# Fused attention, soft mixture of experts and gated MLP: 15 KB more for weights, another order of heads, early clamps on GpSimd

## The chip, the cores and the metric

The kernel runs on one core of a Trainium2 chip. The metric is device time in microseconds, the median of the runs shown. All times of the trace are counted from the first instruction of the profiled execution.

## The reference

Three layers follow each other, all in float32. Attention has 4 batches, 8 heads, 576 tokens and head size 64. Heads 0 to 3 are local (a token sees itself and 31 before it), heads 4 to 7 strided (it sees earlier tokens with the same position modulo 32).

```python
scores = scale * np.matmul(q, k.transpose(0, 1, 3, 2))
scores = np.where(masks[None], scores, -1e9)
attn = softmax(scores);  x = attn @ v            # 2304 tokens x 512

logits = x @ phi                                 # 2304 x 32 slots
slot_input = softmax(logits, axis=0).T @ x       # 32 slots, 4 per expert
slot_out[e] = relu(slot_input[e] @ w1[e]) @ w2[e]    # 8 experts, 512-1024-512
x = softmax(logits, axis=1) @ slot_out

g = x @ w_gate                                   # 512 x 1536
out = (g * sigmoid(g) * (x @ w_val)) @ w_out     # 1536 x 512
```

`w_gate`, `w_val` and `w_out` come as float64; the kernel makes float32 of their bits by itself.

## The kernel before, in words

**Attention.** Two batches at a time (a batch pair, `bp`) and one head make a unit: 16 units, in the order of `HORDER` (heads 0, 1, 4, 5, 2, 3, 6, 7) for both pairs. A unit has three steps of three blocks of 64 tokens. The loop at line 612 takes two steps, n and n+1, in one pass. In pass n TensorE computes the scores of steps n and n+1 (`qk`, line 297, into two banks in turn), the products with v of steps n-4 and n-3 (`pv`, 335) and the transposes of the weights of steps n-2 and n-1 (`tr`, 322). VectorE adds masks and takes maxima (line 303), later divides (341 to 350, writes x); ScalarE takes exponentials (315) and copies transposes (325). Work that comes once per pair of heads hangs at fixed steps in the tables `early`, `side` and `late`: the x-transposes `xtr` (361, with ScalarE's copies 362), the logits (381, a bank per batch pair; strided heads read x with a step), and after the last logits of a batch pair the exponentials over tokens and the slot products `slot` (446). After the last unit a tail of dependent small steps leads to the slot inputs (`weights_a`, `weights_b`, `slot_in`), and the first expert product needs these.

**Loads.** SyncE's queue issues all loads in program order. When the third step of unit u is multiplied with v, `load_v(u + 3)` and `load_qk(u + 4)` are issued and weight halves up to `WTO[u]` (`load_to`, line 635; the list `loads`, line 154, has 70 halves of 512 KB). `load_v` also puts three copies of v on GpSimd (line 278), which shift it to other partitions. Weights lie in `NB` = 14 buffers of two halves; `SHARED` weights go to the buffers of q, k and v when these are done with, `SPEC` weights to buffers of x (tag "x", 6 of them), `SPLIT` to two other places. In the first expert product (line 656, order `W1ORDER`) each weight that is used up frees a buffer, and two more halves are issued; then comes the second product (line 745, order `W2ORDER`).

**Early conversions.** Three tiles of the float64 weights (`PRE`) are loaded first and converted during attention. One conversion (`conv`) has ten parts, in this order: two magnitudes (ScalarE, 198), two clamps (VectorE, 201), two shifts (204), two low words (208), two signs (212, all VectorE). `PRECONV` says at which step how many parts are put at the end of a step's work (`late`): from step 6 on one part a step. So the first conversion has its magnitudes in pass 6, clamps in pass 8, shifts in 10, low words in 12, signs in 14; the second has them in passes 16 to 24, the third from pass 26 to 34.

**Last stage.** The rest of the float64 weights is converted while TensorE multiplies (`half`; its clamp, line 229, is on GpSimd). Program order is the order of each engine's queue.

Of the kernel before, what the change touches and what calls it, by code (L numbers as in the profile page):

```python
# [9 lines left out]
F32 = mybir.dt.float32  # L10
# [4 lines left out]
ALU = mybir.AluOpType  # L15
AX = mybir.AxisListType.X

S = 576
HD = 64
NT = 9  # L20
# [1 line left out]
WID = (96, 80)  # L22
SHIFT = (0, 16)
NEG = -1.0e30
HORDER = (0, 1, 4, 5, 2, 3, 6, 7)
UNITS = [(bp, h) for bp in range(2) for h in HORDER]
C_ID, C_SEL4, C_SELT, C_END = 0, 128, 256, 320
NB = 14
SPEC = (0, 14, 15)
W2ORDER = tuple(range(16, 32, 2)) + tuple(range(17, 32, 2))  # L30
SPLIT = 13
SHARED = W2ORDER[2:5]
WORDER = list(range(1, 11)) + [12, 11] + list(W2ORDER[:2])
REST = list(W2ORDER[5:])
W1ORDER = (1, 2, 3, 4, 0, 13, 5, 6, 7, 14, 8, 15, 9, 10, 12, 11)
PRE = [("g", 0), ("g", 1), ("o", 0)]
PRECONV = [(6, 1), (7, 1), (8, 1), (9, 1), (10, 1), (11, 1), (12, 1), (13, 1), (14, 1), (15, 1), (16, 1), (17, 1), (18, 1), (19, 1), (20, 1), (21, 1), (22, 1), (23, 1), (24, 1), (25, 1), (26, 1), (27, 1), (28, 1), (31, 2), (32, 2), (33, 1), (34, 1), (35, 1)]
ORDER = [("g", 2), ("g", 3), ("o", 1), ("g", 4), ("g", 5), ("o", 2), ("g", 6), ("g", 7), ("o", 3), ("g", 8), ("g", 9), ("g", 10), ("g", 11), ("o", 4), ("o", 5)]
LAG = 3
AHEAD_H = 12  # L40
WT = (0, 0)
ATDVE = ((15, 1),)
# [13 lines left out]
START = (2, 1)  # L56
HEAD = "h g l a0 a1 p2 s0 w1 s1 g p1 w1"
WARM0 = 8
WTO = [6, 8, 10, 12, 14, 16, 18, 20, 22, 24, 26, 28, 31, 38, 42, 43]
NG = 4  # L60
CUTS = [(0, 1, 5, 12), (0, 2, 6, 12), (0, 2, 7, 12), (0, 3, 8, 12), (0, 3, 8, 12)]
MAG_LO = float(np.uint32(0x38000000).view(np.float32))
# [50 lines left out]
def build(ctx: ExitStack, tc: tile.TileContext, cst, phi, qh, kh, vh, w1, w2, wgv, wo, out):  # L113
# [31 lines left out]
    kt = [s0[:, 0:K], s1[:, VW:VW + K], s2[:, VW:VW + K]]  # L145
    vt = [s3[0:96, 0:VW], s1[0:96, 0:VW], s2[0:96, 0:VW]]
    col, par = s2[:, VW + K:VW + K + 128], s2[:, VW + K + 128:VW + K + 144]
    ml, ms = s1[:, VW + K:VW + K + 192], s3[:, VW + S:VW + S + 720]

    wsrc = [w1[j] for j in range(16)] + [w2[j] for j in range(16)]  # L150
    def halves(*js):
        return [(j, hf) for j in js for hf in range(2)]

    loads = halves(*PRE, *WORDER, SPEC[0], *SHARED, SPLIT, *SPEC[1:], *REST)
    at_spec = loads.index((SPEC[0], 0))
    at_split = loads.index((SPLIT, 0))
    wt, gt = {}, {}
# [3 lines left out]
    def load_half(k):  # L161
        for _ in range(k):
            if wn[0] >= NW:
                return
            j, hf = loads[wn[0]]
            if j in SPEC:
                wt[j, hf] = ap_.tile([128, 1024], F32, tag="x", name="wx", bufs=6)
            elif j == SPLIT:
                wt[j, hf] = ap_.tile([128, 2, S], F32, tag="xT", name="wx", bufs=1).rearrange("p a b -> p (a b)")[:, 0:1024] if hf else tmp[:, 0:1024]
            elif hf == 0:  # L170
                a = shared[SHARED.index(j)] if j in SHARED else wp.tile([128, 2048], F32, tag="w", name="w", bufs=NB)
                if j in PRE:
                    gt[j] = a.bitcast(I32)
                wt[j, 0], wt[j, 1] = a[:, 0:1024], a[:, 1024:2048]
            if j in PRE:
                o, i = wt[j, hf].bitcast(I32), (wgv if j[0] == "g" else wo)[j[1], hf].bitcast(I32)
            else:
                o, i = wt[j, hf], wsrc[j][hf]
            SP.dma_start(out=o, in_=i)
            wn[0] += 1  # L180
# [6 lines left out]
    def conv(kind, j):  # L187
        src = gt[kind, j]
        if kind == "g":
            dst = wg[j] = wgs[j % len(wgs)]  # L190
        else:
            dst = wof[j] = wos[j % len(wos)]
        v = [src[:, 1024 * k:1024 * k + 1024].rearrange("p (n t) -> p n t", t=2) for k in range(2)]
        d = [dst[:, 512 * k:512 * k + 512] for k in range(2)]
        di = [a.bitcast(I32) for a in d]

        def mag(k):
            ACT.activation(out=d[k], in_=v[k][:, :, 1].bitcast(F32), func=AF.Abs)

        def clamp(k):  # L200
            DVE.tensor_scalar(out=d[k], in0=d[k], scalar1=MAG_LO, scalar2=MAG_HI, op0=ALU.max, op1=ALU.min)

        def shift(k):
            DVE.tensor_scalar(out=di[k], in0=di[k], scalar1=3, scalar2=0x3FFFFFFF, op0=ALU.logical_shift_left,
                              op1=ALU.bitwise_and)

        def low(k):
            DVE.scalar_tensor_tensor(out=di[k], in0=v[k][:, :, 0], scalar=29, in1=di[k],
                                     op0=ALU.logical_shift_right, op1=ALU.bitwise_or)

        def sign(k):
            DVE.scalar_tensor_tensor(out=di[k], in0=v[k][:, :, 1], scalar=-0x40000000, in1=di[k],
                                     op0=ALU.bitwise_and, op1=ALU.bitwise_or)

        return [(c, fn, k) for c, fn in ((0.0, mag), (0.34, clamp), (0.34, shift), (0.6, low), (0.6, sign))
                for k in range(2)]
# [90 lines left out]
    def expo(u, t):  # L307
        W = WID[UNITS[u][1] // 4]
        sm, mx = sc.pop((u, t))
        o = 288 * ((3 * u + t) % 2)  # L310
        e = tmp[:, o:288 + o].rearrange("p (j k) -> p j k", j=3)
        if W < 96 and u % 4 == 2 and t < 2:
            DVE.memset(e[:, :, 0:96 - W], 0.0)
        for j in range(3):
            ACT.activation(out=e[:, j, 96 - W:96], in_=sm[:, j, 0:W], func=AF.Exp, scale=-1.0, bias=mx[:, j:j + 1])  # L315
        ex[u, t] = e
# [11 lines left out]
    def pv(two):  # L328
        ps = bank("pv", 2)
        for n, (u, t) in enumerate(two):  # L330
            a = at.pop((u, t))
            for j in range(3):
                for b in range(2):
                    o = 65 * (3 * n + j)
                    PE.matmul(out=ps[64 * b:64 * b + 64, o:o + 65], lhsT=a[:, j, 64 * b:64 * b + 64],  # L335
                              rhs=vt[u % AHEAD][:, 65 * (NT * b + 3 * t + j):65 * (NT * b + 3 * t + j) + 65],
                              start=True, stop=True, skip_group_check=True)
        k = 3 * len(two)
        p3 = ps[:, 0:65 * k].rearrange("p (j d) -> p j d", j=k)
        dn = ap_.tile([128, 2, 6, 1], F32, tag="dn", name="dn", bufs=2)[:, :, 0:k]  # L340
        DVE.tensor_scalar_add(dn[:, 0], p3[:, :, HD:HD + 1], 1.0e-9)
        DVE.reciprocal(dn[:, 1], dn[:, 0])
        (u, t), (u1, _) = two[0], two[-1]
        for n, u, t, m in [(0, u, t, 3 * len(two))] if u == u1 else [(0, u, t, 3), (3, u1, 0, 3)]:
            bp, h = UNITS[u]
            y = h // 4
            st, e = divmod(h % 4, 2)
            if t == 0 and e == 0:
                xt[bp, y, st] = ap_.tile([128, NT, 128], F32, tag="x", name="x", bufs=6)
            DVE.tensor_tensor(out=xt[bp, y, st][:, 3 * t:3 * t + m, 64 * e:64 * e + 64], in0=p3[:, n:n + m, 0:HD],  # L350
                              in1=dn[:, 1, n:n + m].to_broadcast([128, m, HD]), op=ALU.mult)

# [11 lines left out]

    lg = {}

    def logits(bp, y, st):
        first, last = (y, st) == (0, 0), (y, st) == (1, 1)
        if first:
            lg[bp] = bank("lg", 1)  # L370
        a = xT.pop((bp, y, st))
        for hf in range(2):
            for b in range(2):
                o = 64 * hf + 32 * b
                if y:
                    rhs = a[:, b, :].rearrange("p (r t) -> p t r", t=18)[:, 9 * hf:9 * hf + 9, :]
                    dst = lg[bp][o:o + 32, 0:288].rearrange("p (t r) -> p t r", r=32)
                else:
                    rhs = a[:, b, 288 * hf:288 * hf + 288]
                    dst = lg[bp][o:o + 32, 0:288]  # L380
                PE.matmul(out=dst, lhsT=phi_t[:, 2 * y + st, :], rhs=rhs, start=first, stop=last,  # L381
                          skip_group_check=True)
# [135 lines left out]
    with tc.manual_schedule():  # L518
# [56 lines left out]
        for bp in range(2):  # L575
            for y in range(2):
                for st in range(2):
                    u = 8 * bp + 4 * st + 2 * y + 1
                    at_step(3 * u + (3 if u == 15 else 5), xT_new, bp, y, st)
                    at_step(3 * u + (3 if u == 15 else 5), xtr, bp, y, st, 0)  # L580
                    at_step(3 * u + 5, xtr, bp, y, st, 1, ("tr", 2) if u in (9, 11) else ("ms", 1))
                    (at_step if u == 15 else lambda n, *a: early.setdefault(n, []).append((a[0], a[1:])))(
                        3 * u + (5 if u == 15 else 7), xtr, bp, y, st, 2)
                    at_step(3 * u + 7, logits, bp, y, st)
# [27 lines left out]
        while n < len(steps) or any(k >= n for k in side):  # L612
            two = (n, n + 1)
            for k in two:
                if k < len(steps):
                    u, t = steps[k]
                    qk(u, t)
            if n == 2:
                load_qk(3)
                load_half(2)  # L620
# [384 lines left out]
```

## Time and profile before

| | |
|---|---|
| time, median of 3 runs | 357.6 us (356.43 to 357.95) |
| profiled execution | 356.76 us, span 355.0 us |
| granted clock of TensorE | 1.00 |
| TensorE busy | 338.2 us (95%) |
| VectorE, ScalarE, GpSimd busy | 219.2, 186.0, 132.7 us |
| DMA | 71.94 MB, mean 203 GB/s |

The span reaches from the first to the last instruction. Busy shares are means over stages that differ: attention to 116 us, the expert products to 152 us, the last stage to the end. PE is TensorE, PEld its weight loads, DVE VectorE, ACT ScalarE, POOL GpSimd, SPq SyncE's queue.

### The profile page before, as it was taken

The numbers are of one execution on the slowest core, as the hardware profiler recorded it, in microseconds if no ns is written. First come the engines' busy times: TensorE is split into PE (matmuls) and PEld (weight loads), VectorE is DVE, ScalarE is ACT, GpSimd is POOL, SyncE is SP. The second block draws the span as 40 slices with busy tenths as digits, with TensorE's granted clock in tenths as the row PEclk, the third lists the DMA queues.
The fourth block names the chain that finished last, engine by engine and source line by source line (L and its number), as shares of the span: only waits on it lengthen the run. The fifth ranks groups of instructions, "written<-read, shape, count | busy, mean of one in ns | idle before, by whom it ended". The sixth has DMA issues, their size and how long they took to land.

```text
span 355.0 us, 7690 instructions
## 1 busy us (share of the span) xinstructions
PE 338.2 (95%) x2856; PEld 244.6 (69%) x2856; DVE 219.2 (62%) x707; ACT 186.0 (52%) x449; POOL 132.7 (37%) x163
## 2 busy tenths in 40 slices
PE   8988999899989999989999999999999999999995
PEld 5866776787747553346777767777776887878774
DVE  4977786765646015468777888797858725242532
ACT  3886979756842002376756555565436634333321
POOL 1514313212110020046484665474526763443331
PEclk9999999999999999999999999999999999999999
DMA  7999999959998999993333334342300003030303
GB/s 205 352 365 404 338 373 361 296 195 349 338 411 310 343 409 408 410 380 127 119 120 118 118 120 123 114 139 99 118 2 2 0 2 118 0 120 2 118 34 143
DMA packets 23397, 71.94 MB, mean 203 GB/s; under 512 B 2624, under 2 KB 3520, under 8 KB 23360
## 3 DMA queue, kind: packets, MB, share of 16 engines
q1 hardware_dynamic: 23072, 71.32, 55.0%
q8 instruction: 22, 0.36, 0.4%
q10 hardware_dynamic: 288, 0.14, 0.1%
q14 instruction: 15, 0.12, 0.1%
HBM read 66.73 MB, written 4.72 MB: 201 GB/s over the span
## 4 chain that ended last, share of the span: by engine, by line
PE 66%; DMA 11%; DVE 9%; ACT 7%; issue 3%; SPq 1%; POOL 1%; DVEq 0%; ACTq 0%; POOLq 0%
PE o L859 35%; DMA w<-in_w 8%; PE sc L297 5%; PE pv L335 5%; PE tr L322 4%; PE gv L825 3%; PE gv L826 3%; PE tr L361 2%; PE lg L381 2%; PE ms L446 2%; DMA s<-in_vh 2%; DVE h L832 2%; DMA g<-in_wgv 1%; PE gv L805 1%; ACT tmp L325 1%
## 5 line engine op out<-in xcount | busy, mean ns | idle before, releaser
L842 POOL TENSOR_TENSOR hl<-h,hh 128x512 fp32r<-128x512 f32 (+1 forms) x60 | 70.9, 1182 | 86.9 <-ACT hh L841 86.8
L859 PE MATMUL o<-woh,hh 128*128 128x512 f32 (+1 forms) x220 | 87.7, 399 | 2.6 <-DVE acc L885 1.4
L859 PE MATMUL o<-wol,hh 128*128 128x512 f32 (+1 forms) x220 | 85.1, 388 | 0.0
L832 DVE TENSOR_TENSOR h<-gv,sg 128x512 f32<-128x512 f32 (+1 forms) x59 | 37.5, 635 | 50.2 <-ACT sg L831 47.3
L859 PE MATMUL o<-woh,hl 128*128 128x512 f32 (+1 forms) x220 | 59.4, 386 | 0.0
L841 ACT CAST hh<-h 128x512 fp32r<-128x512 f32 (+1 forms) x60 | 34.6, 577 | 45.4 <-DVE h L832 45.4
L859 PEld LDWEIGHTS o<-woh,hh 128*128 128x128 f32 x220 | 41.3, 188 | 17.4 <-DVE acc L885 3.4
L278 POOL COPY s<-s 32x390 f32<-32x390 f32 (+1 forms) x48 | 24.2, 504 | 66.7 <-DMA s<-in_vh 52.6
L859 PEld LDWEIGHTS o<-woh,hl 128*128 128x128 f32 x220 | 41.1, 188 | 8.7
L831 ACT ACTIVATE sg<-gv 128x512 f32<-128x512 f32 (+1 forms) x60 | 33.1, 554 | 25.9 <-PE gv L825 25.5
L859 PEld LDWEIGHTS o<-wol,hh 128*128 128x128 f32 x220 | 41.4, 188 | 7.6
L315 ACT ACTIVATE tmp<-tmp,mx 128x96 f32<-128x96 f32 (+1 forms) x144 | 40.9, 363 | 3.8 <-DVE mx L303 3.7
L303 DVE CUSTOM_DVE_ANT_0 tmp<-sc,s 128x96 f32<-128x96 f32 (+1 forms) x144 | 27.9, 245 | 16.4 <-PE sc L297 15.1
L297 PEld LDWEIGHTS sc<-s,s 64*64 64x64 f32 x576 | 24.0, 136 | 10.6 <-issue 5.1
L297 PE MATMUL sc<-s,s 64*64 64x96 f32 (+1 forms) x576 | 28.4, 245 | 2.0 <-DVE mx L303 1.4
L325 ACT COPY tmp<-tr 96x384 f32<-96x384 f32 x47 | 20.2, 476 | 18.7 <-PE tr L322 18.6
L825 PE MATMUL gv<-cs,St 128*128 128x512 f32 (+1 forms) x60 | 25.4, 423 | 0.3 <-DVE St L814 0.3
L229 POOL TENSOR_SCALAR wg<-wg 128x512 f32<-128x512 f32 x20 | 12.3, 614 | 29.1 <-DMA g<-in_wgv 25.4
L335 PE MATMUL pv<-s,tmp 96*64 96x65 f32 x576 | 22.4, 225 | 0.3 <-POOL s L278 0.3
L826 PE MATMUL gv<-cs,St 128*128 128x512 f32 (+1 forms) x59 | 22.3, 379 | 0.3 <-DVE St L814 0.2
L335 PEld LDWEIGHTS pv<-s,tmp 96*64 96x64 f32 x576 | 19.0, 137 | 3.7 <-issue 0.7
L322 PE MATMUL tr<-cst_t,tmp 128*96 128x128 f32 x144 | 21.1, 280 | 0.3 <-ACT xT L362 0.3
(167 smaller groups left out, 460.3 us busy)
## 6 DMA issues: line engine op xcount, KB each, us to landing
w<-in_w SPq DMA_DIRECT2D x50, 512.0 KB, 8.3
g<-in_wgv SPq DMA_DIRECT2D x10, 1024.0 KB, 5.0
g<-in_wo SPq DMA_DIRECT2D x5, 1024.0 KB, 4.9
s<-in_vh SPq DMA_DIRECT2D x16, 292.5 KB, 5.8
out<-osb SPq DMA_DIRECT2D x17, 256.0 KB, 2.2
s<-in_qh SPq DMA_DIRECT2D x15, 288.0 KB, 5.9
s<-in_kh SPq DMA_DIRECT2D x15, 288.0 KB, 6.0
wx<-in_w SPq DMA_DIRECT2D x7, 512.0 KB, 5.7
```

Of the source, the lines that this page charges most:

```text
L297: PE.matmul(out=ps[r, W * j:W * j + W], lhsT=qt[u % AHEAD][r, 64 * i:64 * i + 64], rhs=kt[u % AHEAD][r, c0:c0 + W], start=True, stop=True, ...
L303: DVE.tensor_tensor_reduce(out=sm[:, j, 0:W], in0=ps[:, W * j:W * j + W], in1=mask(y, 3 * t + j), scale=-0.125, scalar=3.0e38, op0=ALU.add ...
L315: ACT.activation(out=e[:, j, 96 - W:96], in_=sm[:, j, 0:W], func=AF.Exp, scale=-1.0, bias=mx[:, j:j + 1])
L322: PE.transpose(ps[0:96, 128 * j:128 * j + 128], e[:, j, :], ident)
L335: PE.matmul(out=ps[64 * b:64 * b + 64, o:o + 65], lhsT=a[:, j, 64 * b:64 * b + 64], rhs=vt[u % AHEAD][:, 65 * (NT * b + 3 * t + j):65 * (N ...
L825: PE.matmul(out=pg[:, 0:n], lhsT=St[f][:, 0:128], rhs=csf[:, t0:t0 + n], start=True, stop=True)
L826: PE.matmul(out=pvv[:, 0:n], lhsT=St[f][:, 128:256], rhs=csf[:, t0:t0 + n], start=True, stop=True)
L831: ACT.activation(out=sg[:, 0:n], in_=pg[:, 0:n], func=AF.Silu)
L832: DVE.tensor_tensor(out=h[:, 0:n], in0=pvv[:, 0:n], in1=sg[:, 0:n], op=ALU.mult)
L841: ACT.copy(a, h)
L842: POOL.tensor_tensor(out=l, in0=h, in1=a.bitcast(F32), op=ALU.subtract)
L859: PE.matmul(out=o[:, 0:c], lhsT=(a, a, l)[i][:, 128 * t:128 * t + 128], rhs=(woh, wol, woh)[i][f][:, c * k:c * k + c], start=(first and i ...
```

## The change

The reservation for dynamic DMA descriptors goes from its default to 1024 bytes, which frees 15 KB per partition. `NB` becomes 15 and tag "x" has 7 buffers; one more second-layer weight is loaded early, the lists and `WTO` follow, and one half of `SPEC` is loaded ahead of the `SHARED` weights. The local heads 2 and 3 come last in both batch pairs; the local masks `ml` move from buffer s1 to s0, and the bank of logits is closed by another pair of heads. The clamps of the early conversions go to GpSimd, and all their parts come two steps (one pass) later: first conversion in passes 8 to 16, second in 18 to 26, third from 28 to 36, with its first clamp at step 31, its second clamp and first shift at step 32, its second shift at step 33. Six filler matmuls are put behind the scores of passes 0, 2 and 4.

```diff
-HORDER = (0, 1, 4, 5, 2, 3, 6, 7)
+HORDER = (0, 1, 4, 5, 6, 7, 2, 3)
-NB = 14
+NB = 15
-SHARED = W2ORDER[2:5]
-WORDER = list(range(1, 11)) + [12, 11] + list(W2ORDER[:2])
-REST = list(W2ORDER[5:])
+SHARED = W2ORDER[3:6]
+WORDER = list(range(1, 11)) + [12, 11] + list(W2ORDER[:3])
+REST = list(W2ORDER[6:])
-PRECONV = [(6, 1), (7, 1), ..., (28, 1), (31, 2), (32, 2), (33, 1), (34, 1), (35, 1)]
+PRECONV = [(k, 1) for k in range(8, 29)] + [(31, 2), (32, 2)] + [(k, 1) for k in range(33, 38)]
+FILL = {0: 3, 2: 2, 4: 1}
-WTO = [6, 8, 10, 12, 14, 16, 18, 20, 22, 24, 26, 28, 31, 38, 42, 43]
+WTO = [6, 8, 10, 13, 15, 17, 20, 22, 24, 27, 29, 31, 34, 41, 45, 46]
-    ml, ms = s1[:, VW + K:VW + K + 192], s3[:, VW + S:VW + S + 720]
+    ml, ms = s0[:, K + 2 * S:K + 2 * S + 192], s3[:, VW + S:VW + S + 720]
-    loads = halves(*PRE, *WORDER, SPEC[0], *SHARED, SPLIT, *SPEC[1:], *REST)
+    loads = (halves(*PRE, *WORDER, SPEC[0]) + [(SPEC[1], 0)] + halves(*SHARED, SPLIT) + [(SPEC[1], 1)] +
+             halves(SPEC[2], *REST))
...
-                wt[j, hf] = ap_.tile([128, 1024], F32, tag="x", name="wx", bufs=6)
+                wt[j, hf] = ap_.tile([128, 1024], F32, tag="x", name="wx", bufs=7)
...
         def clamp(k):
-            DVE.tensor_scalar(out=d[k], in0=d[k], scalar1=MAG_LO, scalar2=MAG_HI, op0=ALU.max, op1=ALU.min)
+            POOL.tensor_scalar(out=d[k], in0=d[k], scalar1=MAG_HI, scalar2=MAG_LO, op0=ALU.min, op1=ALU.max)
...
-        if W < 96 and u % 4 == 2 and t < 2:
+        if W < 96 and u % 8 == 2 and t < 2:
             DVE.memset(e[:, :, 0:96 - W], 0.0)
...
-        first, last = (y, st) == (0, 0), (y, st) == (1, 1)
+        first, last = (y, st) == (0, 0), (y, st) == (0, 1)
...
-                    u = 8 * bp + 4 * st + 2 * y + 1
+                    u = 8 * bp + 4 * st + 2 * (y != st) + 1
...
+            if n in FILL:
+                warm(FILL[n])
...
-    nc = bacc.Bacc("TRN2", target_bir_lowering=False, num_devices=1)
+    nc = bacc.Bacc("TRN2", target_bir_lowering=False, num_devices=1, dynamic_dma_scratch_size=1024)
```

## Rows read from the trace of the kernel before

**Rows 1.** Stages: from:to, length, busy (instructions) by engine, PEclk, DMA, GB/s.
```profile
28.50:58.00 29.50, 28.45 (x471) 21.65 (x471) 21.70 (x132) 23.77 (x73) 7.74 (x17) 1.00 1.00 370
...
74.00:92.00 18.00, 17.76 (x313) 13.83 (x311) 10.82 (x81) 11.99 (x40) 2.80 (x6) 1.00 0.75 266
...
131.80:152.00 20.20, 19.98 (x161) 7.92 (x161) 9.14 (x27) 5.22 (x8) 0.00 (x0) 1.00 1.02 405
...
160.00:355.00 195.00, 188.64 (x874) 144.65 (x872) 124.26 (x201) 95.28 (x184) 99.41 (x98) 1.00 0.25 84
```

**Rows 2.** Waits, 116 to 160 us: engine, line, releaser, total, times, longest.
```profile
PEld sc L656 <- issue: 6.7, 30, 0.2
...
PEld pv L745 <- DMA w<-in_w: 2.9, 4, 1.1
```

**Rows 3.** Timeline, second expert product, weight loads: start, duration, operation, [idle before <-releaser].
```profile
142.50 0.13 PEld L745 LDWEIGHTS pv<-w,hz 128*32 128x32 f32 x4 [0.30 <-issue]
...
147.13 0.14 PEld L745 LDWEIGHTS pv<-w,hz 128*32 128x32 f32 x4 [0.90 <-DMA w<-in_w]
148.41 0.14 PEld L745 LDWEIGHTS pv<-w,hz 128*32 128x32 f32 x4 [1.13 <-DMA w<-in_w]
...
150.97 0.14 PEld L745 LDWEIGHTS pv<-w,hz 128*32 128x32 f32 x4 [0.55 <-DMA w<-in_w]
```

**Rows 4.** Timeline of GpSimd in attention.
```profile
11.90 3.00 POOL L278 COPY s<-s 32x260 f32<-32x260 f32 x6 [0.75 <-DMA s<-in_vh]
14.85 1.05 POOL L563 MEMSET eT<- 128x1152 f32 x1
...
26.77 2.36 POOL L278 COPY s<-s 32x260 f32<-32x260 f32 x3 [6.64 <-DMA s<-in_vh]
...
48.25 1.52 POOL L278 COPY s<-s 32x260 f32<-32x260 f32 x3 [4.32 <-DMA s<-in_vh]
...
70.70 1.52 POOL L278 COPY s<-s 32x260 f32<-32x260 f32 x3 [5.13 <-PE sc L297]
```

**Rows 5.** DMA issues from 41.0 to 41.6 us: count, size, time to landing.
```profile
s<-in_vh SPq DMA_DIRECT2D x1, 292.5 KB, 7.1
```

**Rows 6.** Line 229, the clamp of the last stage: ns min/median/max, first and last start.
```profile
L229 POOL TENSOR_SCALAR wg<-wg x20: 607/614/622, 154.4 to 254.7; 128x512 f32<-128x512 f32 x20
```

**Rows 7.** Timeline, VectorE's conversion parts at the end of passes 12, 22, 32.
```profile
26.71 1.49 DVE L208 SCALAR_TENSOR_TENSOR wg<-w,wg 128x512 int32<-128x512 int32 x2
...
46.23 1.28 DVE L208 SCALAR_TENSOR_TENSOR wg<-w,wg 128x512 int32<-128x512 int32 x2
...
66.95 0.42 DVE L204 TENSOR_SCALAR wo<-wo 128x512 int32<-128x512 int32 x1
```

**Rows 8.** Timeline, scores of passes 14 (second step), 26 and 28.
```profile
28.57 0.71 PE L297 MATMUL sc<-s,s 64*64 64x96 f32 x12 [1.43 <-DVE mx L303]
...
49.40 1.21 PE L297 MATMUL sc<-s,s 64*64 64x96 f32 x24
...
53.47 1.21 PE L297 MATMUL sc<-s,s 64*64 64x96 f32 x24
```

**Rows 9.** Timeline: x-transposes of pass 8; ScalarE in passes 20 and 26.
```profile
19.12 0.55 PE L361 MATMUL tr<-cst_t,x 128*128 128x128 f32 x3 [0.98 <-ACT tmp L325]
...
41.43 0.85 ACT L325 COPY tmp<-tr 96x384 f32<-96x384 f32 x2 [0.24 <-PE tr L322]
...
55.05 1.26 ACT L198 ACTIVATE wo<-w 128x512 f32<-128x512 f32 x2
```

**Rows 10.** Timeline, logits of local heads (23 us) and the last, strided ones.
```profile
23.02 0.69 PE L381 MATMUL lg<-xT,phi_t 128*32 128x288 f32 x8
...
103.19 1.26 PE L381 MATMUL lg<-xT,phi_t 128*32 128x288 f32 x8 [0.57 <-ACT xT L362]
```

**Rows 11.** Timeline, filler matmuls behind the last logits.
```profile
104.39 2.33 PE L516 MATMUL ms<-warm_t 128*128 128x512 bf16 x10
```

**Rows 12.** Waits, 10 to 102 us, VectorE for scores.
```profile
DVE tmp L303 <- PE sc L297: 13.2, 11, 1.8
```

More of the change, by code (lines that the diff above doesn't have):

```diff
@@ L31 @@
 SPLIT = 13
-SHARED = W2ORDER[2:5]
-WORDER = list(range(1, 11)) + [12, 11] + list(W2ORDER[:2])
-REST = list(W2ORDER[5:])
+SHARED = W2ORDER[3:6]
+WORDER = list(range(1, 11)) + [12, 11] + list(W2ORDER[:3])
+REST = list(W2ORDER[6:])
 W1ORDER = (1, 2, 3, 4, 0, 13, 5, 6, 7, 14, 8, 15, 9, 10, 12, 11)
 PRE = [("g", 0), ("g", 1), ("o", 0)]
-PRECONV = [(6, 1), (7, 1), (8, 1), (9, 1), (10, 1), (11, 1), (12, 1), (13, 1), (14, 1), (15, 1), (16, 1), (17, 1), (18, 1), (19, 1), (20, 1), (21, 1), (22, 1), (23, 1), (24, 1), (25, 1), (26, 1), (27, 1), (28, 1), (31, 2), (32, 2), (33, 1), (34, 1), (35, 1)]
+PRECONV = [(k, 1) for k in range(8, 29)] + [(31, 2), (32, 2)] + [(k, 1) for k in range(33, 38)]
 ORDER = [("g", 2), ("g", 3), ("o", 1), ("g", 4), ("g", 5), ("o", 2), ("g", 6), ("g", 7), ("o", 3), ("g", 8), ("g", 9), ("g", 10), ("g", 11), ("o", 4), ("o", 5)]
 LAG = 3
+FILL = {0: 3, 2: 2, 4: 1}
 AHEAD_H = 12
@@ L348, in pv @@
             if t == 0 and e == 0:
-                xt[bp, y, st] = ap_.tile([128, NT, 128], F32, tag="x", name="x", bufs=6)
+                xt[bp, y, st] = ap_.tile([128, NT, 128], F32, tag="x", name="x", bufs=7)
             DVE.tensor_tensor(out=xt[bp, y, st][:, 3 * t:3 * t + m, 64 * e:64 * e + 64], in0=p3[:, n:n + m, 0:HD],
@@ L365, in build, with logits @@
     lg = {}
-    def logits(bp, y, st):
-        first, last = (y, st) == (0, 0), (y, st) == (1, 1)
+    def logits(bp, y, st, halves=(0, 1)):
+        first, last = (y, st) == (0, 0), (y, st) == (0, 1)
         if first:
             lg[bp] = bank("lg", 1)
-        a = xT.pop((bp, y, st))
-        for hf in range(2):
+        a = xT[bp, y, st]
+        for hf in halves:
             for b in range(2):
```

## The prediction

> **What bounds the kernel now.** I read the table of stages first. TensorE is busy in nearly all of every stage and its granted clock is 1.00 throughout, so what counts is which wait ends last in each stage. Four stages matter [rows 1]. From 28.5 to 58 us (attention, batch pair 0) TensorE works 28.45 of 29.5 us and the DMA engines are full as well. From 74 to 92 us the DMA share is only 0.75: about 4.5 us of transfer time are unused there, because the loads have no free buffer. From 131.8 to 152 us (second expert product) the DMA share is 1.02. From 160 us on TensorE works 188.6 of 195 us and DMA is at 0.25; this stage depends only on when it starts, so it moves as a block.
>
> The list of TensorE's waits from 116 to 160 us comes next. The first expert product never waits for a transfer, only for its own issue; the second one waits for weights, 2.9 us in four waits [rows 2]. The timeline shows how much of that is real: a group of four weight loads normally stands 0.30 us ahead of its start, the late ones 0.90, 1.13 and 0.55 [rows 3]. The excess is 0.60 + 0.83 + 0.25 = 1.7 us. So faster weights can give about 1.7 us, 2.9 at the utmost, and whatever makes attention longer now reaches the end nearly whole, because the expert products after it are TensorE's own work.
>
> Attention runs in passes of two steps (pass n is the run of the loop at line 612 that begins with step n; a unit has three steps). In a pass TensorE needs score banks that VectorE has emptied in the pass before, and x-transposes need the x that VectorE writes in the same pass. Every engine's queue runs in program order. On GpSimd this can be seen: the memset of eT needs nothing, is written behind the copies of v, and starts at 14.85, when the last of these ends [rows 4].
>
> **Loads (15 KB more buffer).** Three more 512 KB halves are loaded before attention ends (46 instead of 43 of 70). At the 405 GB/s of the second product a half takes 1.3 us, so the later loads end 3.9 us sooner against the start of the products. The idle DMA time of 74 to 92 us takes them in. TensorE gains what it waits: 1.8 us (0 to 2.9), between the 1.7 above and a few tenths of late starts. One half is now issued ahead of the product that frees its buffer, so SyncE stands there; only weights are behind it. The extra halves of units 3, 6 and 9 stand ahead of later q, k and v in a full queue; a v that lands 7.1 us after its issue [rows 5] is needed about three units later, so nothing but GpSimd notices.
>
> **Clamps on GpSimd.** Six clamps leave VectorE and cost 0.61 us each on GpSimd by the same operation in the last stage [rows 6]. Their cost is not these 0.61 us but where they stand in GpSimd's queue: behind the copies of v (line 278), which wait for their DMA. The shift on VectorE stands one pass later and must wait for the clamp, and everything of VectorE is queued behind it.
>
> First conversion: clamps in pass 10, shift in pass 12. The copies written ahead of the clamps start at 26.77, when v lands, and end between 28.3 (three at 0.5) and 29.13; the clamp ends 0.6 later, at 28.9 to 29.7. VectorE gets there at about 26.7, where now the low words start [rows 7]: a wait of 2.2 to 3.0 us. TensorE itself stands until 28.57 before pass 14's second step [rows 8], which I take for keys that land late and so for independent of this change. That covers most of it. What is left is the x of pass 14, late by about 0.6 us. I take +0.6 (0 to 2.6).
>
> Second conversion: the magnitudes move from pass 16 to 18, and pass 20 has x-transposes. Where the magnitudes stood one pass ahead of such transposes already, TensorE waited 0.98 us for ScalarE. In pass 20 ScalarE has 0.24 us free ahead of its copies, and two magnitudes are 1.26 us [rows 9]: +1.0 us (0 to 1.3). That the first conversion leaves the place with the 0.98 us gives nothing, since TensorE stands until 28.57 anyway. The clamps then stand in pass 20 behind the copies of the v issued just after 41.0 [rows 5], which start at 48.25 and take 1.5 us [rows 4]; the first clamp ends at 50.4, and with the 0.6 us that issue is late by now, at 51.0. VectorE arrives at 46.23 [rows 7] + 1.6 = 47.8 and waits 3.2 us, then does both shifts until about 52. Pass 24's scores need no bank from it, pass 26's do: 49.40 [rows 8] + 1.6 + 0.6 for the logits that are longer in pass 22 now (below) makes 51.6, and the bank comes at 52.5 to 53. Then VectorE still has the low words (1.28 us) ahead of the x for which pass 26's transposes wait, another 1.2 to 1.5 us before pass 28 can start at 53.47 plus all that. I take +2.5 (0 to 3.9).
>
> Third conversion: the second clamp stands in pass 32 behind copies that start at 70.70 and end at 72.2 [rows 4]; it ends at 72.8. The second shift stands in the same pass, where VectorE is at 67 [rows 7]: a wait of over 5 us. TensorE has slot products and logits in these passes that need none of it, and by my count the banks of pass 36 come just in time. +0.5 (0 to 5.3).
>
> What comes back: the magnitudes leave pass 26, where they (55.05, 1.26 us [rows 9]) stand ahead of the copy for which the transposes and logits of pass 28 wait: -0.8 + 0.2 for the one that goes to pass 30. Clamps that no longer stand ahead of the permuted copies of pass 30: -0.3. The other 2 us of VectorE's clamps lie where VectorE is not last: 0.
>
> **A rule weighed against it.** Three copies of v take 2.36 us beside VectorE's low words and 1.52 us in pass 24 [rows 4]. The Trainium skill, SBUF — State Buffer, section "SBUF: two separate sides", says that GpSimd and a VectorE operation that uses both ports shut each other out for a whole instruction. The two rows agree in kind. By that rule a clamp beside a shift would add up to 0.6 us in each conversion, 1.8 us in all; the forecast leaves it out, a rival has it.
>
> **Local heads last, fillers, masks.** Logits of strided heads take 1.26 us and of local ones 0.69 [rows 10]. The last logits, ahead of the whole tail up to the first expert product, become local: -0.6. In batch pair 0 the two change places (pass 22 longer, pass 28 shorter): 0. Masks in another buffer and four small memsets fewer: 0; the shared buffers come free in the old order, one of them some tenths later, with DMA full at that time. Six fillers at 0.23 us (2.33 us for ten [rows 11]) stand in the first 12 us, where TensorE waits for loads: 0, at most 0.4, and the stand until 28.57 covers that too. No idle time that I expect is much longer than the 1.43 us after which the clock stayed at 1.00.
>
> **Sum.** Attention: 0.6 + 1.0 + 2.5 + 0.5 - 0.6 - 0.3 - 0.6 = +3.1 us. Loads: -1.8. Together +1.3 us on the profiled execution of 356.76 us (span 355.0 and 1.8 around it), so 358.1; its time is 0.8 below the median of 357.6 us, and against that I predict 358.9 us.
>
> **Rivals.** (1) TensorE doesn't notice VectorE's waits: only the transposes' 1.0 stays, and -0.6, -0.3, -0.6 and -1.8 make -2.3: 355.3 us. For it: VectorE stands idle for scores up to 1.8 us at a time, 13.2 us in all [rows 12], and v lands sooner when passes are late. Against it: the waits are two to three times that slack. (2) Slower: the third conversion's wait reaches TensorE. It decides from the point where VectorE, 5.3 us late in pass 32, delivers x or banks later than passes 34 and 36 need them; then 5.3 instead of 0.5: +6.1, 363.7 us. For it: clamp and shift of that conversion stand in one pass, behind a v issued in that pass. Against it: the slot products between. (3) GpSimd and VectorE shut each other out as in the rule: +1.8 on the forecast, 360.7 us. (4) The early halves bring nothing, because the weights' queue is full again anyway: +3.1, 360.7 us.
>
> **How the numbers follow.** Chances: forecast 0.50 (its own range 357.0 to 361.0), rival 1 0.29, rival 2 0.10, rival 3 0.06, rival 4 0.05. About 0.5% (1.8 us) is what a measurement of this kernel can tell from no change. Faster than 355.8: most of rival 1, 0.25. Slower than 359.4: 0.4 of the forecast and rivals 2 to 4, 0.40. Between: 0.35. The range of 354.4 to 362.4 takes in rival 1 with a margin, the forecast with its waits at their upper bounds in part, and rivals 3 and 4; rival 2 is left out.
>
> **What would show it.** VectorE idle ahead of line 204 in passes 12, 22 and 32, released by GpSimd's clamp, 2 to 5 us each, with the clamps right behind line 278 on GpSimd: right. The first expert product starting near 119 instead of 116.1 us: attention's +3.1. No wait of line 745 for weights above 0.3 us: the loads' part. The last logits at 0.7 us. I am wrong if VectorE waits there and TensorE has no gap in passes 24 to 28 (rival 1), if line 204 never waits because the clamps run ahead of the copies, or if line 745 still waits for weights.

## The result: 362.7 us, slower by 1.5%

The changed kernel takes 362.66 us (median of 4 runs, 362.01 to 365.37) and the one before 357.3 us beside it: ratio 1.0147, 95% interval 1.0104 to 1.019. The profiled execution took 362.25 us with a span of 360.2 us and a granted clock of 0.999. I had forecast 358.9 us; the time lies just outside the range's upper end of 362.4. The direction and the mechanism were right, the sizes too small. The other three runs show granted clocks of 0.981 to 0.991, so in them some of the loss can be the clock's; in the profiled one it is not, and its loss of 5.5 us against the profiled 356.76 us of before has to be explained without it.

The stages after, from the table of stages (from:to, length, then busy time and instructions of PE, PEld, DVE, ACT, POOL, PEclk, DMA share, GB/s), the first and the last, to be read beside [rows 1]:

```profile
29.60:64.00 34.40, 29.00 (x471) 21.93 (x471) 24.69 (x134) 22.71 (x69) 11.30 (x20) 1.00 0.95 347
...
164.70:360.00 195.30, 189.10 (x874) 145.08 (x874) 124.68 (x201) 95.95 (x184) 99.93 (x98) 1.00 0.24 84
```

The last stage is as long as before (195.3 against 195.0 us). The first stretch runs from pass 14's second step to the scores of pass 30 and holds as many TensorE records, 471, as the first of [rows 1], but is 34.4 us long instead of 29.5 with 5.4 us idle instead of 1.05. The loss is there, in attention.

VectorE's waits for the clamps, from the list of waits, 10 to 110 us (engine, line, releaser, total, times, longest):

```profile
DVE wg L206 <- POOL wg L203: 6.8, 2, 3.5
...
DVE wo L206 <- POOL wo L203: 6.0, 1, 6.0
```

Six of GpSimd's rows explain them (timeline; line 280 copies v, line 203 is the clamp), the counterpart of [rows 4]:

```profile
28.18 1.53 POOL L280 COPY s<-s 32x260 f32<-32x260 f32 x3 [8.33 <-DMA s<-in_vh]
29.80 1.19 POOL L203 TENSOR_SCALAR wg<-wg 128x512 f32<-128x512 f32 x2
...
50.42 1.53 POOL L280 COPY s<-s 32x260 f32<-32x260 f32 x3 [5.17 <-DMA s<-in_vh]
52.04 1.19 POOL L203 TENSOR_SCALAR wg<-wg 128x512 f32<-128x512 f32 x2
...
77.67 1.53 POOL L280 COPY s<-s 32x260 f32<-32x260 f32 x3 [6.32 <-DMA s<-in_vh]
79.28 0.61 POOL L203 TENSOR_SCALAR wo<-wo 128x512 f32<-128x512 f32 x1
```

GpSimd stands idle for 8.33, 5.17 and 6.32 us until a v lands, copies it, and only then clamps. The clamps' inputs had long been there. VectorE's shifts (line 206, timeline) start when the clamp that they need is done, at 30.45, 52.69 and 79.93 us. Before, VectorE was at these places of the program at about 26.7, 46.2 and 67 us [rows 7]:

```profile
30.45 1.15 DVE L206 TENSOR_SCALAR wg<-wg 128x512 int32<-128x512 int32 x2 [3.36 <-POOL wg L203]
...
52.69 1.16 DVE L206 TENSOR_SCALAR wg<-wg 128x512 int32<-128x512 int32 x2 [3.48 <-POOL wg L203]
...
79.93 0.43 DVE L206 TENSOR_SCALAR wo<-wo 128x512 int32<-128x512 int32 x1 [6.01 <-POOL wo L203]
```

What TensorE makes of it (timeline; scores, line 299, of passes 14 second step, 16, 24, 26, 28, 34, 42, and x-transposes, line 363, of passes 26 and 38), to be read beside [rows 8]:

```profile
29.64 0.63 PE L299 MATMUL sc<-s,s 64*64 64x80 f32 x12 [2.29 <-DMA s<-in_kh]
...
33.99 1.05 PE L299 MATMUL sc<-s,s 64*64 64x80 f32 x24
...
50.10 1.21 PE L299 MATMUL sc<-s,s 64*64 64x96 f32 x24
...
54.52 1.21 PE L299 MATMUL sc<-s,s 64*64 64x96 f32 x24 [1.58 <-DVE mx L305]
...
59.73 0.55 PE L363 MATMUL ms<-cst_t,x 128*128 128x128 f32 x3 [1.58 <-DVE x L352]
60.21 1.21 PE L299 MATMUL sc<-s,s 64*64 64x96 f32 x24
...
76.17 1.05 PE L299 MATMUL sc<-s,s 64*64 64x80 f32 x24
...
89.12 0.52 PE L363 MATMUL tr<-cst_t,x 128*128 128x128 f32 x3 [0.87 <-DVE x L352]
...
93.87 1.21 PE L299 MATMUL sc<-s,s 64*64 64x96 f32 x24
```

The middle one is the dearest and is seen twice: first pass 26's score bank is late by 1.58 us, then the x for pass 26's transposes by another 1.58 us, because VectorE puts its low words between. From pass 24 to pass 28 it is 10.1 us, where it was 6.85 before (46.62 to 53.47). The wait of 6.0 us shows mainly as 0.87 us ahead of pass 38's transposes.

The first expert product starts at 123.31 us (116.07 before) and the last stage's first output product at 164.70 (159.57 before). So 7.24 us are lost ahead of the expert products and 2.11 come back in them. The waits of [rows 2] for second-layer weights have shrunk to one short line of the list (115 to 165 us):

```profile
PEld pv L749 <- DMA w<-in_w: 0.3, 1, 0.3
```

### The profile page after: what moved, and what is told of

Read it like the earlier page. It is cut to its first block, busy times and chain, and to the rows that moved or that the text cites. A ratio compares the mean times of both kernels' runs of the same rounds, so it can differ in the third digit from the quotient of the medians.

```text
span 360.2 us, 7701 instructions
## 1 busy us (share of the span) xinstructions
PE 337.4 (94%) x2862; PEld 243.9 (68%) x2862; DVE 217.5 (60%) x697; ACT 187.0 (52%) x449; POOL 136.9 (38%) x169
## 4 chain that ended last, share of the span: by engine, by line
PE 71%; DVE 10%; ACT 7%; DMA 4%; issue 4%; POOL 1%; SPq 1%; DVEq 0%; ACTq 0%; POOLq 0%
PE o L863 35%; PE sc L299 5%; PE pv L749 4%; DMA s<-in_kh 4%; PE sc L660 4%; PE pv L337 4%; PE tr L324 3%; PE gv L829 3%; PE gv L830 3%; PE lg L383 2%; PE ms L448 2%; PE tr L363 2%; DVE h L836 2%; ACT tmp L317 1%; PE gv L809 1%
## 5 line engine op out<-in xcount | busy, mean ns | idle before, releaser
L299 PEld LDWEIGHTS sc<-s,s 64*64 64x64 f32 x576 | 23.2, 133 | 13.9 <-issue 8.7
L239 DVE SCALAR_TENSOR_TENSOR cv<-g,cv 128x512 int32<-128x512 int32 x30 | 20.8, 692 | 0.7
```

Source lines behind the costliest of these rows:

```text
L299: PE.matmul(out=ps[r, W * j:W * j + W], lhsT=qt[u % AHEAD][r, 64 * i:64 * i + 64], rhs=kt[u % AHEAD][r, c0:c0 + W], start=True, stop=True, ...
```

## The experiments

The theory: GpSimd runs in program order, so each clamp inherits the wait for v of the copies written ahead of it, VectorE's queue inherits it from the clamp, and TensorE from VectorE. The rivals: the clamp itself or a shared port is what costs; the moved steps, the heads, the fillers or the loads are what costs.

**e1_clamp_dve**: the changed kernel with the clamps on VectorE again, two steps later as they are.

```diff
-            POOL.tensor_scalar(out=d[k], in0=d[k], scalar1=MAG_HI, scalar2=MAG_LO, op0=ALU.min, op1=ALU.max)
+            DVE.tensor_scalar(out=d[k], in0=d[k], scalar1=MAG_LO, scalar2=MAG_HI, op0=ALU.max, op1=ALU.min)
```

> The changed kernel with the six early clamps back on VectorE; their steps, the fillers, the order of heads and the loads stay as changed. Queue theory (the clamps stand behind the copies of v on GpSimd and hold VectorE 12.9 us in three waits, of which TensorE loses some 5 to 6): the waits ahead of the shifts are gone, the first expert product starts near 118 us instead of 123.3, time 357 us. Place theory (it is the steps, two later, where magnitudes and low words now stand beside x-transposes): start at 121 us or later, time over 360 us. Filler theory (fillers and later keys make most of it): no more than 1 us less, 361.5 us.

Measured: 357.1 us (10 runs, 355.59 to 359.13), ratio to before 0.9993 (0.9954 to 1.0032). 5.6 us less than the changed kernel: the loss goes with the clamps alone. The first expert product started at 120.61 us in the profiled execution, not near 118: this was the slowest of the 10 runs, it stood 3.04 us for keys and fell to a lower clock behind that (last section).

**e3_copies_later**: the clamps stay on GpSimd; the copies of v are written three steps later, into `late`, so that what has its inputs stands ahead of what waits for a transfer.

```diff
-                        load_v(u + 3)
+                        load_v(u + 3, k + 3)      # copies: late.setdefault(k + 3, []).append((copy_v, (u + 3,)))
```

> The changed kernel, clamps on GpSimd at the same steps, but the three copies of v are put into GpSimd's queue three steps after their transfer is issued, so behind the clamps that now wait for them. Queue theory: no wait ahead of the shifts, first expert product near 117.5 us, 356 to 357.5 us. Place theory: over 360 us. Port theory (GpSimd and VectorE shut each other out): part of the loss stays, and VectorE's shifts beside clamps take 0.6 us and more.

Measured: 356.16 us (10 runs, 355.06 to 359.71), ratio 0.9963 (0.9918 to 1.0008). VectorE's waits for line 203 are gone from the list. GpSimd's timeline shows the order turned round, the second conversion's clamps standing in the idle time ahead of the copies (their 2.91 us of waiting is for ScalarE's magnitudes and delays nobody):

```profile
41.75 1.19 POOL L203 TENSOR_SCALAR wg<-wg 128x512 f32<-128x512 f32 x2 [2.91 <-ACT wg L200]
43.55 1.52 POOL L287 COPY s<-s 32x260 f32<-32x260 f32 x3 [0.61 <-PE ms L370]
48.27 1.52 POOL L287 COPY s<-s 32x260 f32<-32x260 f32 x3 [3.21 <-DMA s<-in_vh]
```

Same engine, same clamp, same steps: the place in the queue is the cause. This kernel also prices each wait, since it differs from the changed one in nothing else; it is one execution of each, both with a granted clock of 1.00 all through attention. Its score matmuls of passes 14 (second step), 16, 24, 28, 34 and 42 (timeline):

```profile
28.40 0.63 PE L306 MATMUL sc<-s,s 64*64 64x80 f32 x12 [1.38 <-DMA s<-in_kh]
...
31.71 1.05 PE L306 MATMUL sc<-s,s 64*64 64x80 f32 x24
...
47.81 1.21 PE L306 MATMUL sc<-s,s 64*64 64x96 f32 x24
...
54.66 1.21 PE L306 MATMUL sc<-s,s 64*64 64x96 f32 x24
...
70.63 1.05 PE L306 MATMUL sc<-s,s 64*64 64x80 f32 x24
...
87.31 1.21 PE L306 MATMUL sc<-s,s 64*64 64x96 f32 x24
```

Pass 14 to 16: 3.31 against 4.35 us after; pass 24 to 28: 6.85 against 10.11; pass 34 to 42: 16.68 against 17.70. The three waits cost TensorE 1.04 + 3.26 + 1.02 = 5.3 us.

**e6_conv_only**: the kernel before with only this part: clamps on GpSimd and the new `PRECONV`.

```diff
-PRECONV = [(6, 1), (7, 1), ..., (28, 1), (31, 2), (32, 2), (33, 1), (34, 1), (35, 1)]
+PRECONV = [(k, 1) for k in range(8, 29)] + [(31, 2), (32, 2)] + [(k, 1) for k in range(33, 38)]
...
-            DVE.tensor_scalar(out=d[k], in0=d[k], scalar1=MAG_LO, scalar2=MAG_HI, op0=ALU.max, op1=ALU.min)
+            POOL.tensor_scalar(out=d[k], in0=d[k], scalar1=MAG_HI, scalar2=MAG_LO, op0=ALU.min, op1=ALU.max)
```

> The kernel before with the conversions' part alone: clamps on GpSimd, all parts one pass later; no other loads, order of heads or fillers. Queue theory: the three waits of VectorE come back at about 3, 3.5 and 6 us, the first expert product starts 5 to 6.5 us later, the second product's waits for weights (1.7 us) are covered by that, 361 us. Rival (the waits need the extra loads, which make v late): waits under 2 us, 358 us or less.

Measured: 363.19 us (4 runs, 361.65 to 364.37), ratio 1.016 (1.0115 to 1.0205). This part alone costs 5.7 us, as much as the whole change. Its list of waits (10 to 110 us, then 115 to 165 us):

```profile
DVE wg L204 <- POOL wg L201: 7.7, 2, 4.8
...
DVE wo L204 <- POOL wo L201: 5.0, 1, 5.0
...
PEld pv L745 <- DMA w<-in_w: 2.9, 4, 1.1
```

Attention is longer by more than 7 us, as it is after (first expert product at 123.69 us), but part of it is the clock here: the granted clock was 0.50 to 0.82 in the slices from 30 to 34 and from 54 to 62 us, the second time behind a stand of 3.42 us that the queue itself made, ahead of pass 26's scores (timeline). All four runs have a granted clock of 0.984 to 0.995, so some of the 5.7 us can be the clock's too.

```profile
55.24 2.18 PE L297 MATMUL sc<-s,s 64*64 64x96 f32 x24 [3.42 <-DVE mx L303]
```

The second product still waits 2.9 us for weights; that a later start would cover them was a miss. That fits loads that are issued when the first product frees their buffers and so start later with it; no run here tests that by itself.

**e4_loads_only**: the kernel before with the loads' part alone (15 KB, `NB` 15, 7 buffers of x, lists, `WTO`).

```diff
-NB = 14
+NB = 15
...
-WTO = [6, 8, 10, 12, 14, 16, 18, 20, 22, 24, 26, 28, 31, 38, 42, 43]
+WTO = [6, 8, 10, 13, 15, 17, 20, 22, 24, 27, 29, 31, 34, 41, 45, 46]
...
+    nc = bacc.Bacc("TRN2", target_bir_lowering=False, num_devices=1, dynamic_dma_scratch_size=1024)
```

> The kernel before with the loads' part of the change alone (15 buffers, 7 of tag x, the lists and the plan of loads, the smaller reservation). Prediction's step: line 745 no longer waits for weights, 1.8 us less than before (355.5 us), attention unchanged. Rival: the early halves are hidden anyway or make keys and values late: 357.3 us or more.

Measured: 355.89 us (10 runs, 354.12 to 358.25), ratio 0.9952 (0.9915 to 0.999). The first expert product starts at 117.12, 1.05 us later than before, and the last stage at 158.50, 1.07 sooner: the products give 2.1 us and attention takes half of it back. On the timeline two score matmuls now wait for keys, which stood behind the additional weight halves:

```profile
50.80 0.71 PE L298 MATMUL sc<-s,s 64*64 64x96 f32 x12 [0.62 <-DMA s<-in_kh]
...
63.11 0.63 PE L298 MATMUL sc<-s,s 64*64 64x80 f32 x12 [0.53 <-DMA s<-in_kh]
```

**e5_loads_late**: the same with the additional halves asked for at units 9, 10 and 11 instead of 3, 6 and 9 (edit against e4_loads_only).

```diff
-WTO = [6, 8, 10, 13, 15, 17, 20, 22, 24, 27, 29, 31, 34, 41, 45, 46]
+WTO = [6, 8, 10, 12, 14, 16, 18, 20, 22, 25, 28, 31, 34, 41, 45, 46]
```

> The loads' part alone again, on the kernel before, but the three extra halves are asked for at units 9, 10 and 11, in the stretch where DMA was idle, not at units 3, 6 and 9. With the loads of units 3 and 6 the second steps of passes 26 and 32 waited 0.6 and 0.5 us for keys and the first expert product started 1.0 us later than before. If these keys are what the early halves cost: no such waits, start at 116.1 us, 355.0 us. If the 1.0 us has another cause: start at 117 us, 355.9 us as with the first plan.

Measured: 355.5 us (10 runs, 353.97 to 358.51), ratio 0.9954 (0.9919 to 0.9988). The two waits for keys are gone, but the first product starts at 117.22, no sooner than in e4_loads_only, and the ratio is the same: a miss. The timeline shows where most of the 1.15 us went. A third wait has come, ahead of pass 44's second step:

```profile
91.10 0.63 PE L298 MATMUL sc<-s,s 64*64 64x80 f32 x12 [0.67 <-DVE mx L304]
```

The row names VectorE, but this step needs the keys of unit 15; they were issued at 82.12 us and landed 8.8 us later (6.8 before), at 90.9, while VectorE had emptied the bank by 89.02. From pass 44 to pass 46 it is 4.61 us instead of 3.86. Three weight halves were issued at 78.45 us, ahead of these keys, where it had been two. So the halves that were moved delay later keys instead of earlier ones, in this execution at least.

**e2_no_fill**: the changed kernel without the fillers.

```diff
-FILL = {0: 3, 2: 2, 4: 1}
+FILL = {}
```

> The changed kernel without the six fillers. The second step of pass 14 starts 1.07 us later in the changed kernel than before, behind keys issued 0.3 to 0.5 us apart from before. Queue theory: fillers cost at most this 1.07 us: 361.6 to 362.4 us, VectorE's three waits stay at 3.3, 3.5 and 6 us. Filler theory: 359 us or less. If they cost nothing, as I predicted: 362.7 us.

Measured: 361.37 us (10 runs, 358.66 to 364.32), ratio 1.0112 (1.0066 to 1.0159), 1.3 us below the changed kernel with intervals that overlap. The spread goes with the granted clock: 358.66 us at 1.00, 363.6 to 364.32 at 0.984. VectorE's waits for the clamps were 5.4 us in two and 5.1 in one, against 6.8 and 6.0 after. Not settled by this run; e10_keys_fill does it better below.

**e7_all_mended**: the changed kernel with the copies later, the old `PRECONV`, no fillers and the `WTO` of e5_loads_late; **e8_dve_mended**: the same with the copies in their old place and the clamps on VectorE.

```diff
-PRECONV = [(k, 1) for k in range(8, 29)] + [(31, 2), (32, 2)] + [(k, 1) for k in range(33, 38)]
+PRECONV = [(6, 1), (7, 1), ..., (28, 1), (31, 2), (32, 2), (33, 1), (34, 1), (35, 1)]
-FILL = {0: 3, 2: 2, 4: 1}
+FILL = {}
-WTO = [6, 8, 10, 13, 15, 17, 20, 22, 24, 27, 29, 31, 34, 41, 45, 46]
+WTO = [6, 8, 10, 12, 14, 16, 18, 20, 22, 25, 28, 31, 34, 41, 45, 46]
...
```

> The changed kernel with its parts mended: clamps on GpSimd but copies of v written three steps later, conversions at their old steps, no fillers, extra halves at units 9 to 11; heads in the new order. Queue theory: no waits ahead of shifts, pass 20 without the magnitudes' 1 us, last logits and tail 0.5 us sooner: first expert product at 115.5 us, 354.5 us. If the new order of heads costs as much as it gives: 355.2 us.

> As the run before, but the clamps stay on VectorE and the copies of v at their old place. By my sum the clamps on VectorE cost 0.3 us of TensorE's time: 354.8 us. If clamps off VectorE are worth their 2.6 us of work there: 356.5 us or more.

Measured: 355.42 us (ratio 0.9951, 0.9923 to 0.9978) and 356.06 us (0.995, 0.9921 to 0.9979), 10 runs each. They are 0.64 us apart, with intervals that overlap: the clamps' engine makes no difference that can be measured, once nothing waits ahead of them. Both profiled executions wait some 1.9 us for the keys of pass 14's second step and lose clock behind it.

**e9_keys_sooner**: e7_all_mended with fewer weight halves ahead of the early keys.

```diff
-WTO = [6, 8, 10, 12, 14, 16, 18, 20, 22, 25, 28, 31, 34, 41, 45, 46]
+WTO = [4, 6, 8, 10, 12, 14, 17, 20, 22, 25, 28, 31, 34, 41, 45, 46]
```

> The kernel of e7_all_mended with the early entries of WTO relaxed (4, 6, 8, 10, 12, 14, 17 instead of 6, 8, 10, 12, 14, 16, 18): two weight halves fewer stand ahead of the keys of the early units. Theory (TensorE's stand before pass 14's second step is the queue of loads): with two halves of 1.3 us each fewer ahead of them the keys of unit 5 land up to 2.6 us sooner, the wait of about 1.9 us there goes, the clock stays at 1.00 in the pass after it (3.3 instead of 4.5 us), the first expert product starts near 114.5 instead of 116.85 and the time is 353 to 354 us. Rival (transfers share the engines whatever their order, or the early part of attention is bound by something else): the stand stays within 0.5 us of 1.9, and the time is 355.4 as in e7_all_mended.

Measured: 353.05 us (6 runs, 352.79 to 354.11), ratio 0.9881 (0.9846 to 0.9916): the fastest kernel here, 4.2 us faster than before, and its runs lie within 1.3 us of each other where those of e7_all_mended spread over 3.5. The scores of passes 14, 16 and 32 (second step) on the timeline:

```profile
26.02 1.05 PE L306 MATMUL sc<-s,s 64*64 64x80 f32 x24
...
29.98 1.05 PE L306 MATMUL sc<-s,s 64*64 64x80 f32 x24
...
61.57 0.63 PE L306 MATMUL sc<-s,s 64*64 64x80 f32 x12 [1.64 <-DMA s<-in_kh]
```

Pass 14 now runs both steps without the stand that the prediction took as given, and pass 16 starts at 29.98 instead of 31.97 us before. In this execution 1.64 us of it are lost again to later keys in pass 32, so the first product starts at 115.57 and not near 114.5.

**e10_keys_fill**: e9_keys_sooner with the fillers of the change.

```diff
-FILL = {}
+FILL = {0: 3, 2: 2, 4: 1}
```

> The kernel of e9_keys_sooner with the six filler matmuls of the change behind the scores of passes 0, 2 and 4. Theory of the prediction (fillers lie in idle time): within 0.3 us of e9_keys_sooner. Rival (they delay the early passes, as 361.4 us of e2_no_fill against 362.7 us of the changed kernel hinted): 1.0 to 1.4 us slower, with the first products with v and the passes up to 14 later by as much.

Measured: 354.29 us (9 runs, 353.53 to 355.78), ratio 0.9914 (0.9884 to 0.9943), 1.24 us above e9_keys_sooner; in 50 of the 54 pairs of a run of the one and a run of the other the fillers' run is the slower. On the timeline the fillers stand ahead of transposes and of products with v:

```profile
8.43 0.71 PE L306 MATMUL sc<-s,s 64*64 64x96 f32 x12 [0.21 <-DMA s<-in_kh]
9.08 0.61 PE L525 MATMUL ms<-warm_t 128*128 128x512 bf16 x2
9.52 0.82 PE L331 MATMUL tr<-cst_t,tmp 128*96 128x128 f32 x6
...
11.41 0.39 PE L525 MATMUL ms<-warm_t 128*128 128x512 bf16 x1
11.73 0.92 PE L344 MATMUL pv<-s,tmp 96*64 96x65 f32 x24
```

With the keys there at 8.43, the transposes behind them start at 9.52 instead of 8.99, and pass 16 at 30.79 instead of 29.98: 0.8 us of the 1.24 are seen in this trace. (The rest of this one execution can't be compared: it waits for no keys in pass 32, where e9_keys_sooner lost 1.64 us, and its first product starts at 114.62.)

**e11_old_heads**: e9_keys_sooner with the heads in the old order.

```diff
-HORDER = (0, 1, 4, 5, 6, 7, 2, 3)
+HORDER = (0, 1, 4, 5, 2, 3, 6, 7)
...
-        first, last = (y, st) == (0, 0), (y, st) == (0, 1)
+        first, last = (y, st) == (0, 0), (y, st) == (1, 1)
...
```

> The kernel of e9_keys_sooner with the heads in the order of before (0, 1, 4, 5, 2, 3, 6, 7), the last logits strided again. Theory of the prediction (local logits last shorten the chain to the tail by 0.6 us): 0.6 us slower than e9_keys_sooner, the time from the last x-transposes to the end of the last logits 2.4 instead of 1.8 us. Rival (what is saved there is given back earlier, by longer logits in pass 22 and by magnitudes ahead of other transposes): the same time within 0.2 us, or faster by up to 0.5 us.

Measured: 353.4 us (6 runs, 353.17 to 354.51), ratio 0.9891 (0.9856 to 0.9925), 0.35 us above e9_keys_sooner. The last two logits (timeline), in e11_old_heads:

```profile
95.18 0.69 PE L390 MATMUL lg<-xT,phi_t 128*32 128x288 f32 x8
...
102.02 1.26 PE L390 MATMUL lg<-xT,phi_t 128*32 128x288 f32 x8 [0.57 <-ACT xT L371]
```

and in e9_keys_sooner:

```profile
96.13 1.26 PE L390 MATMUL lg<-xT,phi_t 128*32 128x288 f32 x8
...
102.71 1.27 PE L390 MATMUL lg<-xT,phi_t 128*32 128x288 f32 x8
```

From the last x-transposes to the end of the last logits it is 1.80 us with local heads last and 2.38 with strided ones (102.18 to 103.98, and 100.90 to 103.28): 0.58 us less, close to the 0.6 that I had forecast. But the strided logits have moved to the pass ahead of it and take 1.26 instead of 0.69 us there. From pass 46's scores to the first product it is 22.70 against 22.82 us: 0.1 us is left. The traces side with the rival; the medians, 0.35 us apart, can't decide.

## Why the prediction was wrong, point by point

The lag behind the kernel before, from start to start of the score matmuls of its own trace and the one after, beside the terms of the prediction for that stretch (us):

| stretch | its end before, after | predicted | measured |
|---|---|---|---|
| up to pass 14, second step | 28.57, 29.64 | 0 | +1.07 |
| to pass 16: first conversion's wait | 31.97, 33.99 | +0.6 | +0.95 |
| to pass 24: magnitudes of pass 20, longer logits of pass 22 | 46.62, 50.10 | +1.6 | +1.46 |
| to pass 28: second conversion's wait | 53.47, 60.21 | +2.5 | +3.26 |
| to pass 30: shorter logits, magnitudes gone from pass 26 | 58.38, 64.09 | -1.4 | -1.03 |
| to pass 34: magnitude of pass 30, clamps gone | 69.62, 76.17 | -0.1 | +0.84 |
| to pass 42: third conversion's wait | 86.78, 93.87 | +0.5 | +0.54 |
| to the first expert product: last logits | 116.07, 123.31 | -0.6 | +0.15 |
| attention | | +3.1 | +7.24 |
| expert products: loads | 159.57, 164.70 | -1.8 | -2.11 |

Attention missed the forecast by 4.1 us: 1.15 in the three stretches of the waits (1.7 by the prices of e3_copies_later), 1.07 in the early stretch, 0.94 up to pass 34, 0.75 up to the first expert product, 0.2 elsewhere.

**Mechanism: right.** VectorE stood idle at line 206 for 3.4, 3.5 and 6.0 us; I had worked out 2.2 to 3.0, 3.2 and over 5. The clamps stand behind line 280, and moving the copies away takes it all back. Rival 1 (TensorE doesn't notice) is dead. Rival 2 (the third wait in full) too: of 6.0 us at VectorE TensorE lost 1.0.

**The waits' sizes: the step that failed, together with the three terms that follow.** "I take +0.6", "+2.5" and "+0.5" make 3.6; against e3_copies_later they cost 5.3. The first: it was said to be covered by the stand until 28.57. The keys that end this stand and the v that ends GpSimd's come from the same queue of loads, so they were late together: v's copies started at 28.18 instead of 26.77, and the cover moved but didn't grow. The second: the bank was late by 1.58 us as well as the x behind it, which was seen (0.9 to 1.4 us and 1.2 to 1.5), but 2.5 was taken from the middle, and the x was late by 1.58 us as well. The third: +1.02, half of it hidden in the table because without the wait this stretch is 0.48 us shorter than before.

**The early stretch: not costed at all.** It is +1.07 in this trace. That keys end this stand was taken rightly: they were issued at 20.30 us before and at 20.02 after, and landed 8.1 and 9.5 us later, just ahead of the scores at 28.57 and 29.64. How much of it is fillers can't be read from one execution, since these keys' landing differs from run to run (pass 14's second step starts at 28.20 to 30.12 us over the traces from e1_clamp_dve to e8_dve_mended). The fillers' "0, at most 0.4" is 1.24 us in the pair e9 and e10: I read idle time of the old trace as room, but a filler written behind the scores stands ahead of what the awaited transfer releases.

**The last logits.** The -0.6 is in the trace at its place (1.79 us from the last x-transposes to the end of the last logits, 2.37 before) and is paid back one pass earlier. I counted this exchange in batch pair 0 ("the two change places") and forgot it in batch pair 1.

**Magnitudes.** Pass 20's +1.0 is there (0.92 us of waiting for ScalarE's copy). The +0.2 for the one that goes to pass 30 is too small: that stretch is 0.84 us longer. In it come the exponentials over tokens of batch pair 0, and TensorE waits for their transposes eT, which ScalarE copies (line 436 before, 438 after). Before (first line) it waited 0.40 us; after (the other two) the second magnitude of the third conversion stands ahead of these copies, and it waits 1.58 (its wait just ahead of that is 0.33 us shorter, 0.45 instead of 0.78):

```profile
64.58 0.33 PE L427 MATMUL tr<-cst_t,e 128*128 128x128 f32 x1 [0.40 <-ACT eT L436]
...
69.85 0.65 ACT L200 ACTIVATE wo<-w 128x512 f32<-128x512 f32 x1
...
71.14 0.33 PE L429 MATMUL tr<-cst_t,e 128*128 128x128 f32 x1 [1.58 <-ACT eT L438]
```

Every kernel here with the new `PRECONV` waits 1.00 to 1.58 us at this place, and each with the old steps 0.40. So it is a queue again, ScalarE's ahead of eT, that the term left out.

**Loads.** The products' gain was near (2.11 us against 1.8), by the excess over the normal 0.30 us [rows 3]. That "nothing but GpSimd notices" the early halves was wrong: e4_loads_only shows two waits of TensorE for keys.

**The rule of the two ports.** VectorE's shifts take 0.41 us alone and up to 0.82 us where the second clamp runs beside them, so there is something of rival 3: 0.4 us in each of the two conversions whose shifts overlap a clamp, none in the third. The Trainium skill, SBUF — State Buffer, section "SBUF: two separate sides", has the one engine shut out while the other holds the shared ports; the trace agrees in kind, with less than half of the 1.8 us. Even a first shift of 0.41 us would have left the second one waiting for the second clamp, which ends at 30.99, so less than 0.4 us can be the ports'.

**The parts by medians.** Clamps and steps +5.7 (e6 to before), loads -1.7 (e4 to before), fillers +1.2 (e10 to e9), heads -0.35 (e9 to e11): +4.9 us together, of 5.3 measured by the ratio. Each comes from another pair of kernels, and e6's can hold some of the clock, so the near agreement of the sum may be in part luck.

## What to carry to other kernels

An operation that moves to a less busy engine takes over the waits of everything written ahead of it in that engine's queue: look at what its new neighbours wait for before its duration, and write what waits for a transfer behind what has its inputs. A wait that "is covered" by another is covered only if the two don't come from the same queue; here both were the loads. And ask of every idle stretch in the old profile what ends it: sending two 512 KB halves after the early keys instead of ahead of them was worth more (2.4 us, e7 to e9) than the 15 KB.

## What the hardware showed that I had not expected

An idle TensorE can cost more than its wait. In e1_clamp_dve it stood 3.04 us for keys; the table of stages shows the granted clock behind it at 0.50, the 1.2 GHz level, for some 5 us:

```profile
28.00:30.00 2.00, 0.00 (x0) 0.00 (x0) 0.12 (x2) 0.59 (x3) 1.22 (x3) 0.72 0.99 385
30.00:32.00 2.00, 1.88 (x28) 1.74 (x30) 0.57 (x6) 0.00 (x0) 0.18 (x1) 0.50 1.03 401
32.00:34.00 2.00, 2.00 (x20) 1.54 (x16) 1.18 (x4) 0.47 (x1) 0.54 (x2) 0.50 1.04 408
34.00:36.00 2.00, 2.00 (x19) 1.62 (x20) 1.26 (x2) 1.84 (x6) 1.57 (x2) 0.57 1.08 350
36.00:40.00 4.00, 4.00 (x63) 2.45 (x59) 2.97 (x17) 2.86 (x10) 1.74 (x3) 1.00 0.89 345
```

Pass 14's second step to pass 16 took 5.40 us there instead of 3.31: 2.1 us on top of the wait. The length of the stand alone doesn't decide: after 2.29 us in the changed kernel the clock stayed at 1.00, after 1.92 us in e7_all_mended it was 0.89, 0.50 and 0.76 in the three slices of 2 us from 28 to 34 us, and the same stretch took 4.52 us. In e6_conv_only it fell to 0.50 behind a stand of 1.80 us at this place. What decides is open. The runs of e9_keys_sooner, without this stand, have a granted clock of 0.998 to 1.00 and lie close together; those of e7_all_mended have 0.990 to 1.00, and its two slowest the lowest clocks. So a wait of the queue can cost more than its length too, as the 3.42 us in e6_conv_only show, and the median of a kernel can hold some of that.
